# Twelve subtractions of the first batch on GpSimd, and the last accumulators stored in halves

## The chip, the cores and the metric

The kernel runs on one core of one Trainium2 chip. The core has five engines that run their own instruction streams and wait for each other by semaphores: TensorE (PE, matmuls; PEld is its weight load), VectorE (DVE), ScalarE (ACT), GpSimd (POOL) and SyncE (SP, here only a queue of transfers). Matmuls write to PSUM, all else works in SBUF. The metric is the device time of one execution in microseconds (us). Lower is better.

## The reference

A two-sided attention between tokens and a small state, and a two-layer network behind it. Cut to what matters:

```python
scores = scale * x @ state.T                  # 8 batches, 8 heads, 512 tokens, 32 states, 64 wide
xread  = softmax(scores)  @ state             # for each token
sread  = softmax(scale * state @ x.T) @ x     # for each state
t = concatenate([xread, sread], axis=2)       # 8 x (512 + 32) rows of 512
h = t @ w_in                                  # 512 -> 2048
g = where(h >= 1, h, where(h <= -1, 0, (h + 1) ** 2 / 4))
out = g @ w_out                               # 2048 -> 512
```

All of it is in float32.

## The kernel before, in words

**Tiling.** The network is done in 9 passes: one for the 512 tokens of each of 8 batches, and a last one (`b == B`) for the 256 state rows of all batches. A pass has 8 steps `j` (the last pass 4), each for 256 of the 2048 hidden columns. In a step, `g1` makes two `h` tiles of 128 x 512 in PSUM, from the attention weights and `sw`, which is the state times a chunk of W_in (so `xread` is never formed). ScalarE and VectorE turn `h` into the hidden values `u`: relu (L482), square (L485), bound (L488). `g2` of the step before then multiplies hidden values by W_out and adds into four accumulators `acc`.

**High and low parts.** For float32 accuracy each operand of a matmul is kept as a high part, rounded to the matmul's type by ScalarE, and a low part, which is the value minus the high part. Each product is then three matmuls: high by high, high by low, low by high (L534 to L536 in `g2`). The low parts are subtractions with two inputs: `Hidden.low` for the hidden values (`gl`, L502, both inputs in SBUF), `part_low` for W_out (`wol`, L607, both in SBUF), `sw_low` for `sw` (L436, one input in PSUM), `Attention.rest` (L306).

**The first batch is crowded.** During pass 0 the weights arrive too. Each of the 8 chunks of W_in and 8 tiles of W_out comes in a form that has to be put together: two casts, `high` (L588, ScalarE) and `low` (L575 on VectorE or L580 on ScalarE, as the planner picks), and a `join` (L596, VectorE, both inputs in SBUF). A tile of W_out is then split by `part_high` (L603, ScalarE) and `part_low` (L607). The attention of batches 0 and 1 runs there as well. Between the steps on TensorE stand, one for each step, the transposes and products of the attention's second side (`e2p`, `sr`, `rt`, `sc`), which share with `sw` the single PSUM tile called `mm`. The tile `u` exists once, so a step's relu waits until `gl` of the step before has been made. `gl` and `gh` exist twice.

**What sets the order.** Pass 0 is written as a list of operations, each with engine, a cost, what it comes after, and which buffers it takes. The class `Plan` plays that list forward by its costs, always starting the ready operation with the longest tail behind it, and `emit` writes out the instructions in the order of the planned starts. An engine then runs them strictly in this order. TensorE's order and that of the loads on SP are as written. From pass 1 on the code's own order holds, and nothing of it is changed but the end.

**The end.** After the last step, `store(B, t)` copies each of the two accumulators of the last pass to SBUF (t = 0 on ScalarE, L549; t = 1 on VectorE, L547) and writes it out in four transfers of 32 rows, two from SP and two from ScalarE's queue (L556).

Of the kernel before, what the change touches and what calls it, by code (L numbers as in the profile page):

```python
# [8 lines left out]
F32 = mybir.dt.float32  # L9
# [4 lines left out]
ALU = mybir.AluOpType  # L14
# [8 lines left out]
class Plan:  # L23
# [1 line left out]

    LATE = {"SP": 3.9, "PE": 0.3, "ACT": 0.12, "DVE": 0.12}

    def __init__(self, room, turns, bias):  # L30
        self.bias = bias
# [5 lines left out]
    def op(self, key, engine, cost, run, after=(), take=(), ends=()):  # L37

        after = list(after)
        prior = self.last.get(engine) if engine in ("PE", "SP") else None  # L40
        self.last[engine] = key
        self.ops[key] = [engine, cost, run, after, list(take), list(ends), prior]

    def late(self, k):
        return self.LATE[self.ops[k][0].split("/")[0]]

# [32 lines left out]
    def times(self):  # L79
# [6 lines left out]
        free = dict(self.room)  # L86
        begun, done, where, idle = {}, {}, {}, {e: 0.0 for e in self.LATE}
        events = set()
# [49 lines left out]
def state_exchange_moe(  # L138
# [17 lines left out]
    nc = tc.nc  # L156
    B, P, NT, H, D = x.shape
    S = NT * P
    NS = 32
    DM = H * D  # L160
# [6 lines left out]
    TOK = S + NS  # L167
# [283 lines left out]
    acc = {}  # L451

    class Hidden:
# [39 lines left out]
        def high(self):  # L493
            b, j = self.b, self.j
            gh = work.tile([P, 2, S], F32R, tag="gh", name=f"gh{b}_{j}")
            gl = work.tile([P, 2, S], F32R, tag="gl", name=f"gl{b}_{j}")
            nc.scalar.copy(out=gh, in_=self.u)  # L497
            gs[b, j] = (gh, gl)

        def low(self):  # L500
            gh, gl = gs[self.b, self.j]
            nc.vector.tensor_tensor(out=gl, in0=self.u, in1=gh.bitcast(F32), op=ALU.subtract)  # L502

    def g1(b, j):
        hid = Hidden(b, j)
# [9 lines left out]
    def g2(b, j, half=None):  # L515
        n = n_of[b]
        per = S // n
        nt = n // P
        if b not in acc:
            acc[b] = [ps_acc(f"acc{b}_{t}") for t in range(nt)]  # L520
        gh, gl = gs[b, j]
        last = j == NJ // per - 1
        pairs = [(i, t) for i in range(2 * per) for t in range(nt)]
        if last:
            pairs.sort(key=lambda p: p[1])
        if half is not None:
            pairs = pairs[half * len(pairs) // 2:][:len(pairs) // 2]
        for i, t in pairs:
            f = 2 * per * j + i
            oh, ol = wo[f // 2][:, 0, f % 2], wo[f // 2][:, 1, f % 2]  # L530
            c0 = (i % per) * n + t * P
            lh, ll = (v[:, i // per, c0:c0 + P] for v in (gh, gl))
            a = acc[b][t]
            nc.tensor.matmul(a, lhsT=lh, rhs=oh, start=f == 0, stop=False)  # L534
            nc.tensor.matmul(a, lhsT=lh, rhs=ol, start=False, stop=False)  # L535
            nc.tensor.matmul(a, lhsT=ll, rhs=oh, start=False, stop=f == NF - 1)  # L536
            if last and i == 2 * per - 1:
                store(b, t)
# [3 lines left out]
    def store(b, t):  # L542
        if t == 0:
            outs[b] = rawp.tile([P, NT, DM], F32, tag="raw", name=f"o{b}")
        o = outs[b][:, t]
        if b == B and t % 2:
            nc.vector.tensor_copy(o, acc[b][t])  # L547
        else:
            nc.scalar.copy(out=o, in_=acc[b][t])  # L549
        if b < B:  # L550
            r0 = b * TOK + t * P
            nc.scalar.dma_start(out=out[r0:r0 + P, :], in_=o)
        else:
            for i in range(4):
                r0 = (4 * t + i) * TOK + S
                (nc.sync if i % 2 else nc.scalar).dma_start(  # L556
                    out=out[r0:r0 + NS, :], in_=o[i * NS:(i + 1) * NS]
                )

# [1 line left out]
    parts = {}  # L563
# [26 lines left out]
    def join(kind, c):  # L590
        raw = raws[kind, c]
        if kind == "i":
            a = w32[c].rearrange("p k f -> p (k f)")
        else:
            a = parts[c] = work.tile([P, 1024], F32, tag="tmp", name=f"wf{c}")
        nc.vector.scalar_tensor_tensor(  # L596
            out=a.bitcast(I32), in0=raw[..., 1], scalar=3, in1=raw[..., 0],
            op0=ALU.logical_shift_left, op1=ALU.bitwise_or,
        )

    def part_high(c):
        wo[c] = wop.tile([P, 2, 2, DM], F32R, tag="wo", name=f"wo{c}")
        nc.scalar.copy(out=wo[c][:, 0].rearrange("p a c -> p (a c)"), in_=parts[c])  # L603

    def part_low(c):
        wh, wl = (wo[c][:, i].rearrange("p a c -> p (a c)") for i in range(2))
        nc.vector.tensor_tensor(out=wl, in0=parts[c], in1=wh.bitcast(F32), op=ALU.subtract)  # L607

# [2 lines left out]
    op = plan.op  # L613

    def read(key, cost, f, *a, take=(), after=()):
        op(("dma",) + key, "SP", cost, lambda: f(*a), after=after, take=take)
# [4 lines left out]
    def chunk_ops(c):  # L621

        k = ("i", c)
        read(k, 2.6, fetch, "i", c, take=[("raw", k)])
        op(("high",) + k, "ACT", 1.05, lambda: high("i", c), [("dma",) + k])
        op(("low",) + k, "ACT/DVE", (1.15, 0.75), lambda e: low("i", c, e), [("dma",) + k])
        op(("w", c), "DVE", 1.14, lambda: join("i", c), [("high",) + k, ("low",) + k], ends=[k])

    def out_ops(c):

        k = ("o", c)
        read(k, 2.6, fetch, "o", c)
        op(("high",) + k, "ACT", 1.05, lambda: high("o", c), [("dma",) + k])
        op(("low",) + k, "ACT/DVE", (1.15, 0.75), lambda e: low("o", c, e), [("dma",) + k])
        op(("join", c), "DVE", 1.14, lambda: join("o", c), [("high",) + k, ("low",) + k], take=[("tmp", k)])
        op(("woh", c), "ACT", 0.95, lambda: part_high(c), [("join", c)], ends=[k])
        op(("wol", c), "DVE", 1.14, lambda: part_low(c), [("woh", c)], ends=[k])

    atts = {}

# [46 lines left out]
    hid = {}  # L687

    def hidden_ops(b, j):
        k = (b, j)  # L690
        for i in range(2):
            op(("relu", i) + k, "ACT", 0.58, lambda i=i: hid[k].relu(i), [("p", i) + k], ends=[("h", i) + k],
               take=[("u", ("u",) + k)] if i == 0 else [])
        op(("square",) + k, "ACT", 0.97, lambda: hid[k].square(), [("relu", 0) + k, ("relu", 1) + k])
        for i in range(2):
            op(("bound", i) + k, "DVE", 0.6, lambda i=i: hid[k].bound(i), [("square",) + k], ends=[("h", i) + k])
        op(("gh",) + k, "ACT", 0.97, lambda: hid[k].high(), [("bound", 0) + k, ("bound", 1) + k],
           ends=[("u",) + k], take=[("g", ("g",) + k)])
        op(("gl",) + k, "DVE", 1.14, lambda: hid[k].low(), [("gh",) + k], ends=[("u",) + k])

    def tensor(key, cost, f, after=(), take=(), ends=()):
        op(key, "PE", cost, f, after, take, ends)
# [35 lines left out]
    chunk_ops(0)  # L738
    chunk_ops(1)
    out_ops(0)  # L740
    read(("sb", 1), 1.2, lambda: nc.sync.dma_start(out=sb[:, 1:], in_=state[:, 1:]))
    read(("xn", 0), 2.6, load, "xn", load_xn, 0, take=[("xn", ("xn", 0))])
    chunk_ops(2)
    out_ops(1)
    read(("xt", 1), 2.6, load, "xt", load_xt, 1, take=[("xt", ("xt", 1))])
    for c in range(3, NC):
        chunk_ops(c)
        out_ops(c - 1)
        if c == 5:
            read(("xn", 1), 2.6, load, "xn", load_xn, 1, take=[("xn", ("xn", 1))])  # L750
# [4 lines left out]
    for side in range(2):  # L755
        tensor(("sc", 0, side), 0.6, lambda side=side: att_start(0, side), [("dma", "xt", 0, side)],
               ends=[("xt", 0)])
# [18 lines left out]
    for j in range(NJ):  # L776
        g1_ops(0, j)
        hidden_ops(0, j)
        if j + 1 < NC:
            sw_ops(0, j + 1, 1)  # L780
        if j:
            g2_ops(0, j - 1, 0)
        if j in between:
            between[j]()
        if j == 2:
            att_ops1(1)
            att_ops2(1)
        if j:
            g2_ops(0, j - 1, 1)
# [79 lines left out]
```

## Time and profile before

| | |
|---|---|
| time, median of 3 runs | 663.96 us (663.55 to 664.05) |
| the profiled execution | 664.0 us, its span on the core 662.2 us |
| granted TensorE clock | 1.00 |
| GpSimd | 0.8 us busy, 7 instructions, the last at 1.1 us |
| first `g2` matmul | 29.68 us after the span's start |
| first `sw` matmul of batch 1 | 94.17 us |
| last matmul begins | 657.64 us |
| last copy | 658.07 us, 0.69 long |

How to read it: times inside the profile count from the span's start. A row of a timeline gives start, duration, engine, line, operation, output and inputs, and shape. Instructions of one engine overlap a little at their ends, so the distance from start to start is shorter than the duration. Something in brackets is idle time in front of the instruction and what ended it. The profile's busy time of TensorE holds modelled ends.

### The profile page before, as it was taken

Reading aid. Unit: us, or ns where it says so; the run is one execution under the profiler, and the core shown is the slowest. Engines: PE = TensorE matmul, PEld = TensorE weight load, DVE = VectorE, ACT = ScalarE, POOL = GpSimd, SP = SyncE. Lnnn points to the kernel's source line nnn. Section 1 sums busy time; section 2 is a strip of 40 time slices with the busy share of each in tenths; the row PEclk is TensorE's granted clock in tenths of the full one; section 3 lists DMA queues with packets and bytes.
Section 4 is the critical chain, followed back from the end, with each engine's and each line's share of the span. In section 5 each row is a group of like instructions: output and inputs, shape, how many; then the busy total and the mean of one; then the engine's idle time right before and its main releaser. Section 6 shows DMA issues by size and latency. Waiting matters only on the chain.

```text
span 662.2 us, 10304 instructions
## 1 busy us (share of the span) xinstructions
PE 653.9 (99%) x4442; PEld 514.2 (78%) x4442; DVE 340.3 (51%) x490; ACT 356.5 (54%) x462; POOL 0.8 (0%) x7
## 2 busy tenths in 40 slices
PE   8999999999999999999999999999999999999997
PEld 6677777777787777777787777777778777778896
DVE  5999947623673239433563338433563343333431
ACT  4899847544554446544554447444653454454642
POOL 0000000000000000000000000000000000000000
PEclk9999999999999999999999999999999999999999
DMA  8986103010301003010301002010100000000101
GB/s 359 400 359 249 64 10 119 0 65 0 120 10 64 1 4 124 0 65 0 128 1 64 1 24 105 0 65 0 65 1 1 1 33 32 1 1 1 63 1 33
DMA packets 11085, 43.65 MB, mean 66 GB/s; under 512 B 1312, under 2 KB 1440, under 8 KB 7968
## 3 DMA queue, kind: packets, MB, share of 16 engines
q1 hardware_dynamic: 6096, 34.28, 13.6%
q10 hardware_dynamic: 4944, 8.72, 3.5%
q8 instruction: 35, 0.57, 0.3%
q14 instruction: 10, 0.08, 0.0%
HBM read 34.08 MB, written 8.91 MB: 65 GB/s over the span
## 4 chain that ended last, share of the span: by engine, by line
PE 91%; ACT 5%; DVE 3%; issue 0%; DMA 0%; POOL 0%; SPq 0%; ACTq 0%; POOLq 0%
PE acc L534 19%; PE acc L536 18%; PE acc L535 18%; PE h L477 9%; PE h L479 9%; PE h L478 9%; PE sw L417 5%; PE sc L253 1%; PE sr L350 1%; PE e2p L333 1%; PE warmed L198 1%; ACT u L482 1%; ACT u L485 1%; ACT raw_i L588 1%; DVE w L596 1%; ACT wo L603 0%
## 5 line engine op out<-in xcount | busy, mean ns | idle before, releaser
L534 PE MATMUL acc<-wo,gh 128*128 128x512 f32 x544 | 218.8, 402 | 0.0
L535 PE MATMUL acc<-wo,gh 128*128 128x512 f32 x544 | 212.3, 390 | 0.0
L536 PE MATMUL acc<-wo,gl 128*128 128x512 f32 x544 | 212.2, 390 | 0.0
L482 ACT ACTIVATE u<-h,half 128x512 f32<-128x512 f32 x136 | 93.7, 693 | 219.9 <-PE h L479 202.6
L488 DVE SCALAR_TENSOR_TENSOR u<-u,h 128x512 f32<-128x512 f32 x136 | 87.0, 680 | 206.7 <-ACT u L485 206.7
L534 PEld LDWEIGHTS acc<-wo,gh 128*128 128x128 f32 x544 | 102.1, 188 | 40.1 <-ACT u L482 12.8
L536 PEld LDWEIGHTS acc<-wo,gl 128*128 128x128 f32 x544 | 102.1, 188 | 22.5 <-issue 0.4
L535 PEld LDWEIGHTS acc<-wo,gh 128*128 128x128 f32 x544 | 102.2, 188 | 19.4 <-DVE wo L607 0.3
L502 DVE TENSOR_TENSOR gl<-u,gh 128x1024 fp32r<-128x1024 f32 x68 | 83.2, 1224 | 33.0 <-ACT gh L497 32.0
L497 ACT CAST gh<-u 128x1024 fp32r<-128x1024 f32 x68 | 71.8, 1056 | 50.3 <-DVE u L488 49.9
L485 ACT ACTIVATE u<-u 128x1024 f32<-128x1024 f32 x68 | 72.5, 1065 | 1.3
L417 PE MATMUL sw<-w,sb 64*32 64x256 f32 x1024 | 36.0, 383 | 1.8 <-DVE w L596 1.3
L417 PEld LDWEIGHTS sw<-w,sb 64*32 64x32 f32 x1024 | 15.1, 106 | 17.9 <-issue 8.8
L479 PE MATMUL h<-atl,sw_0h 128*128 128x512 f32 x60 | 23.6, 393 | 0.3 <-DVE atl L306 0.2
L477 PE MATMUL h<-ath,sw_0h 128*128 128x512 f32 x60 | 23.5, 394 | 0.0
L549 ACT COPY o<-acc 128x512 f32<-128x512 f32 x33 | 18.6, 586 | 9.1 <-PE acc L536 9.0
L478 PE MATMUL h<-ath,sw_0l 128*128 128x512 f32 x60 | 23.5, 391 | 0.0
L479 PE MATMUL h<-atl,sw_6h 128*128 128x512 f32 x60 | 23.4, 389 | 0.0
L479 PE MATMUL h<-atl,sw_2h 128*128 128x512 f32 x60 | 23.4, 389 | 0.0
L477 PE MATMUL h<-ath,sw_2h 128*128 128x512 f32 x60 | 23.3, 389 | 0.0
L478 PE MATMUL h<-ath,sw_2l 128*128 128x512 f32 x60 | 23.3, 389 | 0.0
L477 PE MATMUL h<-ath,sw_4h 128*128 128x512 f32 x60 | 23.3, 389 | 0.0
(174 smaller groups left out, 735.0 us busy)
## 6 DMA issues: line engine op xcount, KB each, us to landing
xt<-in_xt_dram SPq DMA_DIRECT2D x16, 512.0 KB, 4.5
raw_i<-in_moe_w_in_dram SPq DMA_DIRECT2D x8, 1024.0 KB, 6.9
raw_o<-in_moe_w_out_dram SPq DMA_DIRECT2D x8, 1024.0 KB, 9.4
xn<-in_x_dram SPq DMA_DIRECT2D x8, 1024.0 KB, 6.4
out_dram<-o ACTq DMA_DIRECT2D x32, 256.0 KB, 2.0
sb<-in_state_dram SPq DMA_DIRECT2D x1, 448.0 KB, 12.6
out_dram<-o SPq DMA_DIRECT2D x4, 64.0 KB, 1.7
out_dram<-o ACTq DMA_DIRECT2D x4, 64.0 KB, 2.0
```

The source lines that it names most:

```text
L417: nc.tensor.matmul(pt[pr * NS:(pr + 1) * NS, hh, i * CI:(i + 1) * CI], lhsT=sb[rows, b, pr], rhs=w32[c + i][rows, pr], start=True, stop=True,)
L477: nc.tensor.matmul(o, lhsT=wh[:, k, sl], rhs=ah[:, k], start=first, stop=False)
L478: nc.tensor.matmul(o, lhsT=wl[:, k, sl], rhs=ah[:, k], start=False, stop=False)
L479: nc.tensor.matmul(o, lhsT=wh[:, k, sl], rhs=al[:, k], start=False, stop=last)
L482: nc.scalar.activation(out=self.u[:, i], in_=self.hs[i], func=AF.Relu, scale=0.5, bias=half)
L485: nc.scalar.activation(out=self.u, in_=self.u, func=AF.Square)
L488: nc.vector.scalar_tensor_tensor(out=self.u[:, i], in0=self.u[:, i], scalar=1.0, in1=self.hs[i], op0=ALU.min, op1=ALU.max,)
L497: nc.scalar.copy(out=gh, in_=self.u)
L502: nc.vector.tensor_tensor(out=gl, in0=self.u, in1=gh.bitcast(F32), op=ALU.subtract)
L534: nc.tensor.matmul(a, lhsT=lh, rhs=oh, start=f == 0, stop=False)
L535: nc.tensor.matmul(a, lhsT=lh, rhs=ol, start=False, stop=False)
L536: nc.tensor.matmul(a, lhsT=ll, rhs=oh, start=False, stop=f == NF - 1)
```

## The change

It has two parts.

The first: in pass 0 the low parts of all 8 W_out tiles (`part_low`) and of the hidden values of every second step (`low` for j = 1, 3, 5, 7) are computed by GpSimd instead of VectorE. The planner gets GpSimd as a fifth engine, with a cost of 2.3 for each of these and 0.15 as the time until others see the result. Since the planner works from costs, much of the order of pass 0 on ScalarE and VectorE is laid anew.

The second: each of the two last accumulators is copied in two halves of 256 columns, one by ScalarE and one by VectorE, and each half is written out by a single transfer of 128 rows, one from ScalarE's queue and one from SP's.

```diff
-    LATE = {"SP": 3.9, "PE": 0.3, "ACT": 0.12, "DVE": 0.12}
+    LATE = {"SP": 3.9, "PE": 0.3, "ACT": 0.12, "DVE": 0.12, "POOL": 0.15}
...
         def low(self):
             gh, gl = gs[self.b, self.j]
-            nc.vector.tensor_tensor(out=gl, in0=self.u, in1=gh.bitcast(F32), op=ALU.subtract)
+            engine = nc.gpsimd if self.b == 0 and self.j % 2 else nc.vector
+            engine.tensor_tensor(out=gl, in0=self.u, in1=gh.bitcast(F32), op=ALU.subtract)
...
         o = outs[b][:, t]
-        if b == B and t % 2:
-            nc.vector.tensor_copy(o, acc[b][t])
-        else:
+        if b < B:
             nc.scalar.copy(out=o, in_=acc[b][t])
-        if b < B:
             r0 = b * TOK + t * P
             nc.scalar.dma_start(out=out[r0:r0 + P, :], in_=o)
         else:
-            for i in range(4):
-                r0 = (4 * t + i) * TOK + S
-                (nc.sync if i % 2 else nc.scalar).dma_start(
-                    out=out[r0:r0 + NS, :], in_=o[i * NS:(i + 1) * NS]
-                )
+            rows = out.rearrange("(b t) d -> b t d", b=B)[4 * t:4 * t + 4, S:S + NS]
+            lo, hi = slice(0, DM // 2), slice(DM // 2, DM)
+            nc.scalar.copy(out=o[:, lo], in_=acc[b][t][:, lo])
+            nc.vector.tensor_copy(o[:, hi], acc[b][t][:, hi])
+            nc.scalar.dma_start(out=rows[:, :, lo], in_=o[:, lo])
+            nc.sync.dma_start(out=rows[:, :, hi], in_=o[:, hi])
...
     def part_low(c):
         wh, wl = (wo[c][:, i].rearrange("p a c -> p (a c)") for i in range(2))
-        nc.vector.tensor_tensor(out=wl, in0=parts[c], in1=wh.bitcast(F32), op=ALU.subtract)
+        nc.gpsimd.tensor_tensor(out=wl, in0=parts[c], in1=wh.bitcast(F32), op=ALU.subtract)
...
-        op(("wol", c), "DVE", 1.14, lambda: part_low(c), [("woh", c)], ends=[k])
+        op(("wol", c), "POOL", 2.3, lambda: part_low(c), [("woh", c)], ends=[k])
...
-        op(("gl",) + k, "DVE", 1.14, lambda: hid[k].low(), [("gh",) + k], ends=[("u",) + k])
+        op(("gl",) + k, "POOL" if j % 2 else "DVE", 2.3 if j % 2 else 1.14, lambda: hid[k].low(), [("gh",) + k], ends=[("u",) + k])
```

The line numbers after the change are one lower for the lines behind `store` (L588 becomes L587, L596 becomes L595, L603 becomes L602, L607 becomes L606) and one higher for those between `low` and `store` (L502 becomes L503, L534 to L536 become L535 to L537).

GpSimd's queue after its start-up rows, all of it new. `wo` is the low part of a W_out tile (0 to 7 in this order), `gl` that of the hidden values of step 1, 3, 5 or 7, `wf` a joined tile:

```order
L606 TENSOR_TENSOR wo_276<-wf_247,wo_276 128x1024
L606 TENSOR_TENSOR wo_364<-wf_357,wo_364 128x1024
L503 TENSOR_TENSOR gl_1_420<-u_1_300,gh_1_419 128x1024
L606 TENSOR_TENSOR wo_446<-wf_434,wo_446 128x1024
L606 TENSOR_TENSOR wo_485<-wf_478,wo_485 128x1024
L606 TENSOR_TENSOR wo_609<-wf_588,wo_609 128x1024
L503 TENSOR_TENSOR gl_3_627<-u_3_533,gh_3_626 128x1024
L606 TENSOR_TENSOR wo_643<-wf_630,wo_643 128x1024
L606 TENSOR_TENSOR wo_714<-wf_688,wo_714 128x1024
L606 TENSOR_TENSOR wo_736<-wf_724,wo_736 128x1024
L503 TENSOR_TENSOR gl_5_813<-u_5_716,gh_5_812 128x1024
L503 TENSOR_TENSOR gl_7_943<-u_7_898,gh_7_942 128x1024
```

`gl` of step 3 stands behind the low part of W_out tile 4, which step 4 needs.

ScalarE at the end of step 0, before, from the high cast of W_in chunk 2 (`raw_i_198`) on; `gh_0` is the high part of step 0, `wo` that of W_out tile 0, `e` the copy of `e2p`, `u_1` the relus of step 1:

```order
L588 ACTIVATE raw_i_198<-raw_i_198 128x1024
L497 CAST gh_0_306<-u_0_222 128x1024
L603 CAST wo_310<-wf_247 128x1024
L337 COPY e_0_237<-e2p_286 128x1024
L482 ACTIVATE u_1_298<-h_1_0_299,half 128x512
L482 ACTIVATE u_1_298<-h_1_1_312,half 128x512
L432 CAST sw_2h<-sw_2_327 128x512
L485 ACTIVATE u_1_298<-u_1_298 128x1024
```

and after:

```order
L602 CAST wo_276<-wf_247 128x1024
L587 ACTIVATE raw_i_198<-raw_i_198 128x1024
L497 CAST gh_0_309<-u_0_222 128x1024
L337 COPY e_0_237<-e2p_287 128x1024
L587 ACTIVATE raw_o_208<-raw_o_208 128x1024
L432 CAST sw_2h<-sw_2_327 128x512
L482 ACTIVATE u_1_300<-h_1_0_301,half 128x512
L482 ACTIVATE u_1_300<-h_1_1_313,half 128x512
L602 CAST wo_364<-wf_357 128x1024
L485 ACTIVATE u_1_300<-u_1_300 128x1024
```

The cast of W_out tile 0 now comes first, and that of tile 1 (`wo_364`) stands in front of the square of step 1.

VectorE behind the bound of step 1 (the L488 pair on `u_1`), before; `wf` and `w` are joins of W_out tiles and W_in chunks, L575 the `low` casts:

```order
L488 SCALAR_TENSOR_TENSOR u_1_298<-u_1_298,h_1_1_312 128x512
L596 SCALAR_TENSOR_TENSOR wf_399<-raw_o_208 128x1024
L596 SCALAR_TENSOR_TENSOR w_3_90<-raw_i_268 128x1024
L502 TENSOR_TENSOR gl_1_402<-u_1_298,gh_1_401 128x1024
L607 TENSOR_TENSOR wo_417<-wf_399,wo_417 128x1024
L358 TENSOR_TENSOR rs_433<-sr_366,r_0_323 128x128
L575 TENSOR_SCALAR raw_i_320<-raw_i_320 128x1024
L596 SCALAR_TENSOR_TENSOR wf_446<-raw_o_295 128x1024
L596 SCALAR_TENSOR_TENSOR w_4_91<-raw_i_320 128x1024
```

and after:

```order
L488 SCALAR_TENSOR_TENSOR u_1_300<-u_1_300,h_1_1_313 128x512
L595 SCALAR_TENSOR_TENSOR w_3_90<-raw_i_268 128x1024
L358 TENSOR_TENSOR rs_422<-sr_367,r_0_321 128x128
L595 SCALAR_TENSOR_TENSOR wf_434<-raw_o_296 128x1024
L574 TENSOR_SCALAR raw_i_325<-raw_i_325 128x1024
L574 TENSOR_SCALAR raw_o_360<-raw_o_360 128x1024
L595 SCALAR_TENSOR_TENSOR w_4_91<-raw_i_325 128x1024
L595 SCALAR_TENSOR_TENSOR wf_478<-raw_o_360 128x1024
L436 TENSOR_TENSOR sw_3l<-sw_3_453,sw_3h 128x512
```

The two subtractions are gone, the joins have closed up, and a `low` cast of W_out tile 3 that ScalarE did has come over.

VectorE behind the bound of step 3, after:

```order
L488 SCALAR_TENSOR_TENSOR u_3_533<-u_3_533,h_3_1_547 128x512
L574 TENSOR_SCALAR raw_o_541<-raw_o_541 128x1024
L275 TENSOR_TENSOR z_492<-z_492,m_1_493 128x512
L595 SCALAR_TENSOR_TENSOR wf_630<-raw_o_541 128x1024
L574 TENSOR_SCALAR raw_i_568<-raw_i_568 128x1024
L271 TENSOR_REDUCE m_1_493<-z_492 128x16
L595 SCALAR_TENSOR_TENSOR w_7_94<-raw_i_568 128x1024
```

where two joins, `gl` of step 3 and the low part of W_out tile 4 stood before. L275 and L271 are the first side of batch 1's attention, moved up.

## The prediction

> **What bounds the kernel now.** I read the page first, then the busy time by stretches, then the chain that ended last, then the rows of each engine in the stretch in question. The page says TensorE, and that GpSimd is unused:
>
> ```profile
> PE 653.9 (99%) x4442; PEld 514.2 (78%) x4442; DVE 340.3 (51%) x490; ACT 356.5 (54%) x462; POOL 0.8 (0%) x7
> ```
>
> The average hides the first batch. The columns below are stretch, its length, and busy us of PE, PEld, DVE, ACT, POOL, then clock and DMA:
>
> ```profile
> 21.00:35.00 14.00, 13.06 (x152) 9.32 (x151) 13.39 (x20) 13.85 (x20) 0.00 (x0) 1.00 0.94 379
> 35.00:50.00 15.00, 14.98 (x97) 10.56 (x103) 14.03 (x20) 14.19 (x19) 0.00 (x0) 1.00 0.93 373
> 50.00:62.00 12.00, 12.00 (x79) 8.96 (x80) 11.62 (x14) 12.00 (x16) 0.00 (x0) 1.00 0.84 330
> 62.00:80.00 18.00, 17.86 (x168) 13.39 (x166) 17.90 (x30) 15.12 (x19) 0.00 (x0) 1.00 0.18 60
> ```
>
> In these 59 us VectorE is busy for 13.39 + 14.03 + 11.62 + 17.90 = 56.9. TensorE is dense as well, so three engines are full at once, and every us by which VectorE or ScalarE hands over later moves the rest of the program, in which TensorE is never idle. The chain of waits shows how tight it is; it leaves VectorE for good only here:
>
> ```profile
> 60.45 1.10 DVE wf L596
> 61.55 0.55 issue
> 62.10 0.69 DVE sw_5l L436
> ```
>
> There is little to win. From the first `g2` on, TensorE waits twice, about 0.3 us each: for the low part of W_out 0 (the page's row of that matmul's weights names it last), and at 62.84.
>
> ```profile
> L535 PEld LDWEIGHTS acc<-wo,gh 128*128 128x128 f32 x544 | 102.2, 188 | 19.4 <-DVE wo L607 0.3
> ```
>
> So what counts is whether the new order delivers on time.
>
> **GpSimd's price.** No row shows a subtraction on GpSimd. The nearest of its own rows, and VectorE's rows for the work itself:
>
> ```profile
> 1.10 0.29 POOL masks.py:199 TENSOR_SCALAR_AFFINE_SELECT ident<-ident 128x128 f32<-128x128 f32 x1
> ```
> ```profile
> 25.75 0.69 DVE L575 TENSOR_SCALAR raw_o<-raw_o 128x1024 int32<-128x1024 uint32 x1
> 26.36 1.22 DVE L596 SCALAR_TENSOR_TENSOR w<-raw_i 128x1024 int32<-128x1024 int32 x1
> 27.49 1.22 DVE L502 TENSOR_TENSOR gl<-u,gh 128x1024 fp32r<-128x1024 f32 x1
> ...
> 28.91 1.20 DVE L607 TENSOR_TENSOR wo<-wf,wo 128x1024 fp32r<-128x1024 f32 x1
> ```
>
> Eight times the 128 columns of the first row are 0.29 x 8 = 2.3 us with one input; with two, at worst, 4.6. From below, VectorE's own 1.22. I take **2.3**, the row of the same engine. The Trainium skill (GPSIMD Engine Reference, Performance versus the Vector engine) gives 4497 ns for 2048 elements of a two-input add; half of that is an estimate of 2.25 us, which no run here shows yet.
>
> **Do the two engines get in each other's way?** No row of before has both computing at once. What VectorE's rows show, from start to start: 1024 elements with one input take 26.36 - 25.75 = 0.61 us, with two inputs 27.49 - 26.36 = 1.13 us. Input elements go by at the same rate, so VectorE already draws two streams from SBUF in both forms. I take it as likelier that a third reader has to wait its turn than that it has a way of its own. So my forecast is that a GpSimd subtraction and a VectorE instruction of those two kinds (two SBUF inputs, or the fast one-input form) **take turns**, each whole. Instructions that read PSUM (L436, L488), reductions and transposes go on beside GpSimd. The Trainium skill says the same of this change (SBUF — State Buffer, Who interferes with whom): a VectorE instruction with two SBUF inputs, or in a two-port mode, and a GpSimd instruction that reads SBUF exclude each other for the whole instruction, whoever starts first. By that rule the subtractions cost more than they save; whether it holds here, only the next trace can show.
>
> **The change, place by place, with turns.** I lay the new orders out with the durations of before. Twelve subtractions leave VectorE (12 x 1.13 = 13.6 us). The planner also gives VectorE four `low` casts that ScalarE did (0.61 each, against 1.12 from start to start on ScalarE, 55.61 to 56.73 below).
>
> *Place A, step 0.*
>
> ```profile
> 25.06 1.20 ACT L588 ACTIVATE raw_i<-raw_i 128x1024 f32<-128x1024 f32 x1
> 26.10 1.08 ACT L497 CAST gh<-u 128x1024 fp32r<-128x1024 f32 x1
> 27.04 1.08 ACT L603 CAST wo<-wf 128x1024 fp32r<-128x1024 f32 x1
> ```
> ```profile
> 29.09 0.67 PE L417 MATMUL sw<-w,sb 64*32 64x256 f32 x16 [0.45 <-ACT e L337]
> ...
> 30.51 0.40 PE L536 MATMUL acc<-wo,gl 128*128 128x512 f32 x1
> ```
>
> The cast of W_out tile 0 now goes first: 25.06 + 1.08 = 26.14. GpSimd lets the fast cast at 25.75 end (26.44) and holds until 28.74. VectorE's join of `w` 2 is ready at 27.2 (cast, then 1.2 for the input), but starts at 28.74 and ends at 29.9, so `sw` 2 moves from 29.09 to 29.95. `gl(0,0)` follows at 30.2 (two small rows, 0.3) and ends at 31.4, wanted at 30.51. **A = +0.9.**
>
> *Place B, `gl(0,1)`.* After `gl(0,0)` VectorE does a fast cast and the join of `wf` 1 (30.2 + 1.13 + 0.61 + 1.2 = 33.1); only then can ScalarE cast W_out tile 1 (34.2), and the square of step 1 now stands behind that cast. GpSimd holds from 34.2 to 36.5. Then VectorE has a run without a gap: `w` 3, a 0.2 us row, `wf` 2, two fast casts, `w` 4, `wf` 3 = 4 x 1.13 + 0.2 + 2 x 0.61 = 5.9, to 42.4. `gh(0,1)` is ready about 38.3, so `gl(0,1)` on GpSimd waits for the end of the run: 42.4 to 44.7. It is wanted by this matmul, moved by A:
>
> ```profile
> 40.74 0.40 PE L536 MATMUL acc<-wo,gl 128*128 128x512 f32 x1
> ```
>
> 40.74 + 0.9 = 41.6. **B = +3.1.** Behind it on GpSimd wait the low parts of tiles 2 and 3; the single `u` tile stays taken, so ScalarE's relu of step 2 waits too.
>
> *The transpose at 53.39.* ScalarE now has a `low` cast in front of `sw_4h`:
>
> ```profile
> 51.40 0.61 ACT L432 CAST sw_4h<-sw 128x512 fp32r<-128x512 f32 x1
> ...
> 54.58 1.20 ACT L588 ACTIVATE raw_o<-raw_o 128x1024 f32<-128x1024 f32 x1
> 55.61 1.31 ACT L580 ACTIVATE raw_o<-raw_o,offset 128x1024 int32<-128x1024 uint32 x1
> 56.73 1.11 ACT L497 CAST gh<-u 128x1024 fp32r<-128x1024 f32 x1
> ```
> ```profile
> 52.35 0.68 DVE L436 TENSOR_TENSOR sw_4l<-sw,sw_4h 128x512 fp32r<-128x512 f32 x1
> ```
> ```profile
> 53.39 0.27 PE L364 MATMUL rt<-ident,rs 128*128 128x128 f32 x1
> ```
>
> It delays `sw_4l` by 1.1; the `mm` tile came free at 52.35 + 0.68 = 53.03, 0.36 before its next user. **+0.7**, with turns or without.
>
> *Place C, `gl(0,3)`.* GpSimd's queue has the low part of W_out 4 ahead of it. That cast now stands where ScalarE was at 54.58; moved by 0.9 + 3.1 + 0.7 = 4.7 it ends at 60.4, GpSimd holds until 62.7, VectorE's run (fast cast, subtract of 512 columns, join, fast cast: 0.61 + 0.6 + 1.13 + 0.61) lasts until 65.7, `gl(0,3)` until 68.0. Wanted here:
>
> ```profile
> 60.24 0.40 PE L536 MATMUL acc<-wo,gl 128*128 128x512 f32 x1
> ...
> 62.31 0.39 PE L536 MATMUL acc<-wo,gl 128*128 128x512 f32 x1
> 62.84 1.09 PE L333 MATMUL e2p<-ident,e 128*128 128x128 f32 x8
> ```
>
> 60.24 + 4.7 = 64.9: 3.0 late, of which 0.3 replaces the wait at 62.84 (matmuls of this form follow each other every 0.23, so this one could have begun at 62.54). **C = +2.7.**
>
> *Place D, the `mm` tile for `sr(1)`.* From the end of `gl(0,3)`, T, VectorE does a join, a fast cast, then while GpSimd holds (2.3) only `sw_5l`, then a fast cast, a join (to T + 5.8), the pair of L488 with two small rows (7.4), and subtract, sum, join, `gl(0,4)` (10.9). GpSimd holds until T + 13.2; then normalise, 0.3 of small rows, transpose, `sw_6l`: T + 15.4. TensorE needs the tile at:
>
> ```profile
> 72.89 1.10 PE L350 MATMUL sr<-xn,e 128*32 128x64 f32 x64
> ```
>
> That is 72.89 - 60.24 - 0.3 = 12.35 after T. **D = +3.0.** Later GpSimd subtractions (steps 5 and 7) come behind the loads and joins, where VectorE has gaps again, and have slack.
>
> *The tail.* Columns of the DMA rows: minimum, median and maximum ns of an issue, first and last start; then us to landing, of L556 and of L552.
>
> ```profile
> 7.21 0.78 DVE L260 STREAM_TRANSPOSE z<-sc 128x256 f32<-128x256 f32 x2 [6.31 <-PE sc L253]
> ...
> 658.07 0.69 DVE L547 COPY o<-acc 128x512 f32<-128x512 f32 x1 [5.42 <-DMA out_dram<-o]
> ```
> ```profile
> L556 SPq DMA_DIRECT2D out_dram<-o x4: 315/386/415, 656.0 to 659.2; - x4
> DMA to landing us min/median/max: 1.6/1.9/2.0
> ```
> ```profile
> DMA to landing us min/median/max: 2.0/2.0/4.3
> ```
>
> The last copy shrinks from 0.69 to about 0.4 (the 256-wide rows), and each queue issues one transfer for the last tile instead of two: the last issue moves from 659.2 to 658.55. A transfer of 128 rows lands in 2.0 (L552) against 1.9. So -0.65 + 0.15 = **-0.5** (bounds -0.8, and +0.5 if 1 KB rows land slower than any row here).
>
> **Sum.** 0.9 + 3.1 + 0.7 + 2.7 + 3.0 - 0.5 = +9.9. The profiled execution took 664.0 us (span 662.2, 1.8 around it), the median of three is 663.96, so either base gives **673.9**. With 1.22 per subtraction about +4.5 remains (668.5); with 4.6 about twice the sum.
>
> **Rivals.**
> 1. *Side by side, no turns* (not slower). A: the low part of W_out 0 is done at 26.2 + 2.3 = 28.5, and TensorE's wait for it goes, -0.3; `gl(0,1)` is in time; the transpose +0.7; C: tile 4 at 55.0 to 56.1, its low part to 58.4, `gl(0,3)` to 60.7, wanted at 60.64, so +0.1, less 0.3; D up to +0.4; tail -0.5: between -0.3 and +0.1, **664.0**. It decides if a subtraction on GpSimd lasts about 2.3 while VectorE's rows stay at 1.13. For it: VectorE is relieved of 13.6 us. At 4.6 us each, `gl(0,3)` alone would be 4.7 late.
> 2. *Turns, but GpSimd always gets in first.* Eleven subtractions before 82 us hold VectorE for 25.3; it is relieved of 11 x 1.13 = 12.4 and given 2.4 of casts: +15.3, and VectorE was full. **678.8.**
> 3. *Only GpSimd waits, VectorE is never held.* A -0.3; B +2.5 (the run starts 1.5 earlier and the demand 1.2 earlier); transpose +0.7; C +0.5; D +0.5; tail -0.5: **667.4.**
> 4. *A real gain*: all waits of TensorE (0.6) and the tail at its best (0.8) are won: **662.5.** It needs a GpSimd about as fast as VectorE.
>
> **How the numbers follow.** A run of this kernel can tell 0.2% (1.3 us) from nothing. Forecast 0.36, rival 2 0.16, rival 3 0.16, rival 1 0.28, rival 4 0.04. Slower: 0.36 + 0.16 + 0.16, and 0.03 of rival 1 with a slower GpSimd = 0.71; same 0.25; faster 0.04. The range runs from rival 1's lower part, 663.6, to 681, rival 2 with a somewhat longer subtraction. The forecast's own range is 668.5 to 678.
>
> **What would show it.** Turns: VectorE rows of L595, L503 or L574 that last 2 to 3 us where a GpSimd row overlaps them, and PE waits on `gl` at about 42 and 65 us of 3 us each. Side by side: those rows stay at 1.22 and 0.69, and `sw` of batch 1 starts at about 94 as before. The tail: one issue per queue after the last copy, its end 0.5 closer to the last matmul. The forecast is wrong if GpSimd rows lie over two-input VectorE rows without either growing.

## The result: slower by 2.8%, and the profile after

The changed kernel takes 682.08 us (681.52 to 683.1, five runs), the kernel before beside it 663.96 us. The ratio is 1.0282, with a 95% interval of 1.0269 to 1.0295 (the two medians alone give 1.0273). The profiled execution took 682.88 us, its span is 681.1 us. The direction was as forecast; the time is 8.2 us above the forecast of 673.9 and 1.1 us above the upper end of its range. One execution of a later kernel, `e1_tail_only`, took 3701.75 us with TensorE slow throughout, and its figure leaves that execution out.

First the page's line of busy times after the change, in us, with shares of the span and counts:

```profile
PE 658.3 (97%) x4442; PEld 517.4 (76%) x4442; DVE 347.0 (51%) x483; ACT 353.2 (52%) x459; POOL 33.2 (5%) x19
```

Twelve subtractions left VectorE, 12 x 1.13 = 13.6 us by the rows of before, and yet its busy time rose from 340.3 to 347.0. That is the first thing to look into. VectorE's and GpSimd's rows in one stretch after the change (start, duration, engine, line, operation, output and inputs, shape):

```profile
61.52 2.63 DVE L574 TENSOR_SCALAR raw_o<-raw_o 128x1024 int32<-128x1024 uint32 x1
64.08 2.85 DVE L275 TENSOR_TENSOR z<-z,m 128x512 f32<-128x512 f32 x1
...
70.32 2.85 DVE L574 TENSOR_SCALAR raw_o<-raw_o 128x1024 int32<-128x1024 uint32 x1
```
```profile
61.19 2.42 POOL L606 TENSOR_TENSOR wo<-wf,wo 128x1024 fp32r<-128x1024 f32 x1 [11.33 <-ACT wo L602]
63.56 2.82 POOL L503 TENSOR_TENSOR gl<-u,gh 128x1024 fp32r<-128x1024 f32 x1
69.23 3.39 POOL L606 TENSOR_TENSOR wo<-wf,wo 128x1024 fp32r<-128x1024 f32 x1 [2.85 <-ACT wo L602]
```

The cast of L574 takes 0.69 us by itself, the subtraction of L275 0.68. Here each lasts until the GpSimd row beside it is over (61.19 + 2.42 = 63.61) and then does its own work. So the engines do take turns, each whole. But it is VectorE that stands still inside its run of work. The second GpSimd row starts at 63.56, in the middle of a run of VectorE: GpSimd didn't wait for a gap.

Where TensorE waited, from 20 to 112 us after the change (waiting instruction, what released it; us in total, times, longest):

```profile
PE e2p L333 <- DVE sw_5l L436: 4.8, 1, 4.8
PE sc L253 <- DVE sw_3l L436: 3.4, 1, 3.4
PE sr L350 <- DVE sw_6l L436: 2.4, 1, 2.4
PE sw L417 <- DVE r L339: 1.3, 1, 1.3
PE acc L537 <- POOL gl L503: 0.8, 1, 0.8
```

Three of the waits are for `sw_3l`, `sw_5l` and `sw_6l`, VectorE's subtractions out of PSUM (which VectorE reads as well as SBUF, L436 and L488) that set the single `mm` tile free for the second attention, that of batch 1. Only 0.8 us is a wait for GpSimd's own result, and in this stretch VectorE and ScalarE wait for none. The first `sw` matmul of batch 1 begins at 110.65 us against 94.17: of the 18.9 us by which the span grew, 16.5 are lost in the first batch. The other 2.4 are at the end: from the start of the last tile's first copy to the end of the span were 662.2 - 658.1 = 4.1 us, and now 681.1 - 674.6 = 6.5:

```profile
674.17 0.39 PE L537 MATMUL acc<-wo,gl 128*128 128x512 f32 x1
674.60 0.37 ACT L554 COPY o<-acc 128x256 f32<-128x256 f32 x1 [2.35 <-PE acc L537]
675.00 0.55 ACTq L556 DMA_DIRECT2D out_dram<-o  x1
675.00 0.42 DVE L555 COPY o<-acc 128x256 f32<-128x256 f32 x1 [2.29 <-ACT o L554]
675.46 0.54 SPq L557 DMA_DIRECT2D out_dram<-o  x1
```

Each copy is shorter, as forecast, but the two run one behind the other. So the last issue starts 675.46 - 674.17 = 1.29 us after the last matmul starts, against 659.2 - 657.64 = 1.56 before: 0.3 us are gained. That issue is over at 676.0, and the writes themselves then take until about 679.5.

The trace also shows TensorE's clock at half behind the long waits. Busy us in two pieces after the wait for `sc` (stretch, length, then PE, PEld, DVE, ACT, POOL, clock, DMA share, GB/s):

```profile
46.90:48.00 1.10, 1.02 (x16) 0.23 (x16) 0.62 (x2) 1.10 (x2) 0.52 (x1) 0.50 0.75 313
48.00:50.00 2.00, 2.00 (x19) 0.94 (x4) 1.50 (x4) 1.41 (x2) 1.86 (x1) 0.50 1.03 434
```

`sc` takes 1.96 us in place of 1.09. So from the trace alone there are four suspects: the turns, the new order of the planner, the halved clock, and the writes at the end.

### The profile page after: what moved, and what is told of

It reads as the page before. It is cut to its first block, busy times and chain, and to the rows that moved or that the text cites. A ratio compares the mean times of both kernels' runs of the same rounds, so it can differ in the third digit from the quotient of the medians.

```text
span 681.1 us, 10318 instructions
## 1 busy us (share of the span) xinstructions
PE 658.3 (97%) x4442; PEld 517.4 (76%) x4442; DVE 347.0 (51%) x483; ACT 353.2 (52%) x459; POOL 33.2 (5%) x19
## 4 chain that ended last, share of the span: by engine, by line
PE 87%; DVE 8%; ACT 2%; issue 2%; POOL 0%; ACTq 0%; DVEq 0%; POOLq 0%
PE acc L535 18%; PE acc L537 17%; PE acc L536 17%; PE h L477 9%; PE h L479 9%; PE h L478 9%; PE sw L417 4%; DVE w L595 1%; DVE wf L595 1%; PE sr L350 1%; PE sc L253 1%; DVE raw_o L574 1%; PE e2p L333 1%; PE warmed L198 1%; DVE gl L503 1%
## 5 line engine op out<-in xcount | busy, mean ns | idle before, releaser
L535 PE MATMUL acc<-wo,gh 128*128 128x512 f32 x544 | 220.1, 405 | 0.0
L537 PE MATMUL acc<-wo,gl 128*128 128x512 f32 x544 | 213.1, 392 | 0.8 <-POOL gl L503 0.8
L536 PE MATMUL acc<-wo,gh 128*128 128x512 f32 x544 | 213.3, 392 | 0.0
L488 DVE SCALAR_TENSOR_TENSOR u<-u,h 128x512 f32<-128x512 f32 x136 | 87.1, 680 | 208.5 <-ACT u L485 208.5
L535 PEld LDWEIGHTS acc<-wo,gh 128*128 128x128 f32 x544 | 102.9, 189 | 41.0 <-ACT u L482 12.8
L537 PEld LDWEIGHTS acc<-wo,gl 128*128 128x128 f32 x544 | 102.7, 189 | 24.4 <-POOL gl L503 1.2
L536 PEld LDWEIGHTS acc<-wo,gh 128*128 128x128 f32 x544 | 102.9, 189 | 19.2
L503 DVE TENSOR_TENSOR gl<-u,gh 128x1024 fp32r<-128x1024 f32 x64 | 80.5, 1258 | 33.6 <-ACT gh L497 32.6
L606 POOL TENSOR_TENSOR wo<-wf,wo 128x1024 fp32r<-128x1024 f32 x8 | 21.7, 2722 | 54.4 <-ACT wo L602 54.4
L477 PE MATMUL h<-ath,sw_6h 128*128 128x512 f32 x60 | 23.4, 389 | 0.0
```

The lines of the kernel that those rows point to most:

```text
L477: nc.tensor.matmul(o, lhsT=wh[:, k, sl], rhs=ah[:, k], start=first, stop=False)
L488: nc.vector.scalar_tensor_tensor(out=self.u[:, i], in0=self.u[:, i], scalar=1.0, in1=self.hs[i], op0=ALU.min, op1=ALU.max,)
L503: engine.tensor_tensor(out=gl, in0=self.u, in1=gh.bitcast(F32), op=ALU.subtract)
```

## The experiments

Differences are against the kernel before on the same chip (663.3 to 663.5 us).

### Order and engine apart

Four kernels. The first has only the change's `store`:

```diff
 # kernel before
-            for i in range(4): ... (32 rows x 512 columns each)
+            nc.scalar.dma_start(out=rows[:, :, lo], in_=o[:, lo])
+            nc.sync.dma_start(out=rows[:, :, hi], in_=o[:, hi])
```

> The kernel before with the change's last copies and writes alone (two halves of 256 columns on two engines, one transfer of 4 x 32 rows of 1 KB for each half). If the trace of the changed kernel is read rightly, the end behind the last matmul grows from 4.1 to 6.4 us, and the time goes from 664.0 to 666.3 (665.8 to 666.8). By the prediction's term for the tail it is 0.5 us faster: 663.5.

Measured: 665.8 us, ratio 1.0031 (1.0019 to 1.0044), so 2.3 us slower by the medians. The second is the changed kernel with the `store` of before:

> The changed kernel with the tail of before: only the twelve subtractions are on GpSimd. If the parts add up, 682.1 - 2.3 = 679.8 (679.0 to 680.6). If the tail costs more or less beside a late first batch, another number.

Measured: 679.64 us, 16.2 slower. 16.2 + 2.3 = 18.5 against 18.1 for the whole change: the parts add up to within 0.4 us. From here on the tail is that of before. The third keeps the new plan but runs its subtractions on VectorE, the fourth keeps the old plan and runs them on GpSimd:

```diff
 # e3: the changed kernel's plan (cost 2.3 on "POOL")
-        nc.gpsimd.tensor_tensor(out=wl, ...)
+        nc.vector.tensor_tensor(out=wl, ...)
 # e4: the plan of before (cost 1.14 on "DVE")
-        nc.vector.tensor_tensor(out=wl, ...)
+        nc.gpsimd.tensor_tensor(out=wl, ...)
 # and gl of steps 1, 3, 5, 7 likewise
```

> The order of instructions that the changed kernel's planner makes, with all twelve subtractions on VectorE again, and the tail of before. Theory of turns: without GpSimd rows no VectorE row is held, VectorE does 1.13 us each as before, so 664 within 1.5 us. Rival, that the new order and not the engine costs the time: 676 or more.

> The order of before, with the twelve subtractions on GpSimd, and the tail of before. Theory of turns: VectorE's rows are held to 2.4 to 3 us beside GpSimd rows here too, and sc, e2p and sr of the second attention come late, so 674 to 684. Rival, that the new order costs the time: 664 to 666.

Measured: 672.39 us (+8.9) and 669.89 us (+6.4). Neither theory had that. The turns alone don't make 16.2 in the old order, and the new order costs time without any GpSimd row. What TensorE waits for with the old order:

```profile
PE sw L417 <- ACT e L322: 1.8, 1, 1.8
PE acc L536 <- POOL wo L608: 0.8, 1, 0.8
```

The others are 0.7 us at most and spread out; none for `e2p` or `sc` is over 0.4 us.

### Shorter holds, a warm clock, no subtractions, and the forms by themselves

All three kernels have the new order and the tail of before. In the first each GpSimd subtraction is cut in four; in the second TensorE has matmuls in front of its three waits (the first column of `pad` holds 0.5, so they add to one row of an accumulator and not only zeros); in the third GpSimd only fills the twelve low parts with zeros, so the subtractions are left out:

```diff
 # e5
-        nc.gpsimd.tensor_tensor(out=wl, in0=parts[c], in1=wh.bitcast(F32), op=ALU.subtract)
+        for q in range(4):
+            s = (slice(None), slice(q * 256, q * 256 + 256))
+            nc.gpsimd.tensor_tensor(out=wl[s], in0=parts[c][s], in1=wh[s].bitcast(F32), op=ALU.subtract)
 # e6
+    nc.tensor.matmul(acc[b][0][:PAD, :P], lhsT=pad, rhs=ident, start=False, stop=False)  # 14, 20, 5 times
 # e7
-        nc.gpsimd.tensor_tensor(out=wl, in0=parts[c], in1=wh.bitcast(F32), op=ALU.subtract)
+        nc.gpsimd.memset(wl.bitcast(F32), 0.0)
```

> The new order and the tail of before, each of the twelve subtractions on GpSimd cut into four of 256 columns. If the two engines take turns by whole instructions, a VectorE row waits for a quarter (0.6 to 0.75 us) and not for 2.4 us: rows that were 2.6 to 3.4 us long fall to 1.3 to 2, and the time falls from 679.6 to 668 to 674. If a GpSimd subtraction slows VectorE by traffic, in whatever pieces, or the new order is the cost, it stays at 678 to 682.

> The subtractions on GpSimd in the new order with the tail of before, and TensorE kept at work where it idled: matmuls that add zeros, 14 ahead of sc, 20 ahead of e2p and 5 ahead of sr of the second attention. If the halved clock behind each idle stretch is a cost of its own, sc, e2p and the matmuls behind them keep a pitch of 0.23 us, and 679.6 falls by some 5 us to 674.5 (673.5 to 676). If that time is covered by something else that is late, 678.5 to 680.

> The new order and the tail of before, with GpSimd filling the twelve low parts with zeros in place of the subtractions, so that the low parts of W_out and of every second step's values in the first batch are left out. Theory of turns: without a two-input GpSimd row no VectorE row is held, and the new order by itself costs nothing: 664 within 1.5 us. Rival, that the order of the new planner costs the time (672.4 with all on VectorE): 670 or more. If a fill holds VectorE as a subtraction does, for its shorter time: 665 to 669, with VectorE rows of 1.5 to 2.2 us beside it.

Measured: quarters 675.66 us (+12.4), warm 679.5 us, no subtractions 665.14 us (+1.9).

The third shows that with VectorE really relieved the new order costs only 1.9 us. (A fill is also done sooner than a subtraction, but in the changed kernel only 0.8 us was a wait for a GpSimd result.) The first shows that the length of the single GpSimd instruction matters, though less than expected: TensorE now waits 1.7 us for a `gl` from GpSimd. The second refutes the clock as a cost. The busy times of `e2_subs_only` by stretch, then those of `e6_warm`:

```profile
36.00:52.00 16.00, 12.57 (x69) 8.05 (x68) 14.67 (x16) 10.72 (x14) 8.33 (x3) 0.79 0.83 329
52.00:74.00 22.00, 17.17 (x100) 12.42 (x99) 20.88 (x19) 17.25 (x22) 8.61 (x3) 0.97 0.49 192
74.00:88.00 14.00, 12.76 (x79) 9.75 (x80) 13.90 (x19) 7.80 (x10) 5.77 (x2) 0.80 0.00 1
```
```profile
36.00:52.00 16.00, 15.69 (x108) 12.09 (x107) 14.69 (x16) 10.80 (x14) 8.34 (x3) 1.00 0.87 343
52.00:74.00 22.00, 19.64 (x132) 14.92 (x131) 21.07 (x21) 17.15 (x22) 8.58 (x3) 1.00 0.46 183
74.00:88.00 14.00, 11.42 (x96) 8.68 (x98) 13.90 (x19) 7.80 (x10) 5.75 (x2) 1.00 0.00 1
```

The clock went from 0.79, 0.97 and 0.80 to 1.00 in all three stretches, and `sr` begins at 87.61 us in place of 87.74. VectorE's column explains it: 14.67 of 16 us, 20.88 of 22, 13.90 of 14, and nearly the same in `e6_warm`. VectorE, its held time included, is the bound through these 52 us. What TensorE won by its clock went into the added matmuls and into new waits, of which two for `gl` are 1.1 and 1.0 us.

The fourth kernel measures the turns by themselves: ten forms on VectorE, three of each, first alone, then beside GpSimd's subtractions, fills and copies of 1024 columns.

```python
# v = VectorE, g = GpSimd; tiles of 128 x 1024, pq in PSUM (512), tiny 16 columns
L37 v.tensor_tensor(vo, va, vb)          L38 the same, 512 columns
L39 v.tensor_scalar(vo, va)              L40 v.tensor_scalar(tiny, tiny)
L41 v.tensor_tensor(vo, pq, va), 512     L43 v.transpose(vo, pq), 512
L64 g.tensor_tensor(go, ga, gb)          L65 g.memset(go)          L66 g.tensor_copy(go, ga)
```

> No part of the reference is computed: ten forms of VectorE instruction, three of each, first alone, then beside GpSimd subtractions of 1024 columns, then beside GpSimd fills, then beside GpSimd copies. By the traces so far, beside subtractions: two SBUF inputs 1.13 and 0.6 us grow to 3 to 3.5, one SBUF input (1024 and 16 columns) to 2.4 to 3; PSUM input, reduction and transposes keep their 0.6 to 0.7. A rival, that everything on VectorE is held: all ten forms by over 1 us. Beside fills: nothing is held, if only GpSimd's reads take the turn.

Its timeline of VectorE, three instructions to a row: alone, then beside subtractions (from 29.43), fills (from 116.03) and copies (from 159.15). Then GpSimd's rows of subtractions and fills:

```profile
3.53 3.73 DVE L37 TENSOR_TENSOR vo<-va,vb 128x1024 f32<-128x1024 f32 x3
7.29 2.15 DVE L38 TENSOR_TENSOR vo<-va,vb 128x512 f32<-128x512 f32 x3
9.47 2.15 DVE L39 TENSOR_SCALAR vo<-va 128x1024 f32<-128x1024 f32 x3
11.53 0.59 DVE L40 TENSOR_SCALAR tiny<-tiny 128x16 f32<-128x16 f32 x3
12.03 2.13 DVE L41 TENSOR_TENSOR vo<-pq,va 128x512 f32<-128x512 f32 x3
...
29.43 8.20 DVE L38 TENSOR_TENSOR vo<-va,vb 128x512 f32<-128x512 f32 x3
37.67 8.20 DVE L39 TENSOR_SCALAR vo<-va 128x1024 f32<-128x1024 f32 x3
45.79 4.74 DVE L40 TENSOR_SCALAR tiny<-tiny 128x16 f32<-128x16 f32 x3
50.45 2.13 DVE L41 TENSOR_TENSOR vo<-pq,va 128x512 f32<-128x512 f32 x3
...
116.03 3.75 DVE L37 TENSOR_TENSOR vo<-va,vb 128x1024 f32<-128x1024 f32 x3
...
121.99 3.77 DVE L39 TENSOR_SCALAR vo<-va 128x1024 f32<-128x1024 f32 x3
...
163.65 4.29 DVE L38 TENSOR_TENSOR vo<-va,vb 128x512 f32<-128x512 f32 x3
167.97 4.29 DVE L39 TENSOR_SCALAR vo<-va 128x1024 f32<-128x1024 f32 x3
```
```profile
24.99 90.80 POOL L64 TENSOR_TENSOR go<-ga,gb 128x1024 f32<-128x1024 f32 x36
...
117.36 41.55 POOL L65 MEMSET go<- 128x1024 f32 x40
```

Beside subtractions a VectorE instruction of 0.6 us (L38, L39) comes round every 8.20 / 3 = 2.73 us: 2.1 us of one GpSimd subtraction, then its own 0.6. Neither starves in these two forms: one instruction of each, in turn. The form with a PSUM input is not touched (2.13 and 2.13), nor are reductions and transposes. A fill (41.55 / 40 = 1.04 us each) leaves the two-input form alone (3.75 against 3.73) but holds the fast one-input form by 0.54 us each (3.77 against 2.15). That was not expected of a fill; in `e7_no_subs` such holds sum to 2.0 us (the table below), beside the 1.9 us by which it is slower. The Trainium skill (SBUF — State Buffer, Who interferes with whom) states these pairs: two SBUF inputs against a GpSimd instruction that reads, the two-port forms against any. The runs agree, and add that with both queues full the lock passes to and fro.

### The account of VectorE, tested forward

If VectorE is the bound up to `sw_6l`, its end must follow from what VectorE has to do before it. The table is worked out from the traces: "held" is the sum, over VectorE's rows from 20 us up to the end of `sw_6l`, of what each row is longer than the median row of its form in the kernel before. "Subtractions" are those of `gl` and `wo` that VectorE did itself until then, "casts" the `low` casts it did.

| kernel | order | end of `sw_6l` | held | subtractions | casts |
|---|---|---|---|---|---|
| before | old | 72.31 | 0.2 | 11 | 8 |
| e4, GpSimd | old | 77.39 | 12.4 | 3 | 8 |
| e3, VectorE | new | 80.85 | 0.4 | 13 | 12 |
| e7, fills | new | 73.57 | 2.0 | 3 | 12 |
| e5, quarters | new | 84.16 | 9.6 | 3 | 12 |
| e2, GpSimd | new | 87.68 | 16.9 | 3 | 12 |
| changed kernel | new | 87.87 | 16.9 | 3 | 12 |

From e7 to the changed kernel the end moves by 14.3 us and the held time by 14.9. Until then GpSimd has begun ten subtractions: 1.7 us of VectorE for each, where VectorE does one in 1.13. And the new order has already spent what it counted on: VectorE's own subtractions until `sw_6l` fall from 11 to 3, 8 x 1.13 = 9.0 us, but 71 instructions stand before it and not 67, the planner having put four more casts and a good part of the second attention's softmax there. So the whole held time lands on `sw_6l`. In the old order the 9.0 us stay free: e4's end moves by 5.1 us, 2.7 of them busy time of VectorE up to there (53.0 against 50.3) and 2.4 idle time. The account has a limit: it takes VectorE's idle time as given. That is 2.0 to 4.5 us up to `sw_6l` in six of the seven kernels but 7.2 in e5, whose end moves 3.0 us more against e7 than its held time.

Two kernels test that account: the old order with quarters, and a planner that is told the truth.

```diff
 # e10: kernel before, each subtraction as four of 256 columns on GpSimd (as in e5)
 # e11: the change's subtractions on GpSimd, the tail of before, and
-        op(("wol", c), "POOL", 2.3, lambda: part_low(c), ...)
+        op(("wol", c), "DVE", 1.7, lambda: part_low(c), ...)
 # and gl of odd steps likewise
```

> The order and the tail of before, the twelve subtractions on GpSimd, each in four of 256 columns. By the account of VectorE's time up to sw_6l (held 12.4 us with whole subtractions in this order against 9.1 us taken away; quarters held 9.6 where whole ones held 16.9): held some 7, so 663.5 to 666.5. Rival, that GpSimd's own results come later in quarters and become the wait: 668 or more, with TensorE waiting for wo or gl from GpSimd.

> The subtractions whole on GpSimd and the tail of before, but the planner reckons them as 1.7 us of VectorE (what they cost it by the held rows) in place of 2.3 us of GpSimd. If it is the planner's filling of time that VectorE does not have that puts the products sw late, the conversions stay on ScalarE and the time is 666 to 671 (669.9 with the order of before). If the order does not matter: 678 to 681.

Measured: `e10_old_quarters` 668.43 us (+5.1), `e11_told` 667.63 us (+4.3). In `e11_told` 11.9 of the 16.2 us have gone although the subtractions are on GpSimd as before; `sw_6l` ends at 75.48 with 9.4 us held and 7 casts. VectorE is idle for 8.4 us up to there, so it is no longer the bound throughout. Its waits:

```profile
PE e2p L333 <- DVE sw_5l L436: 0.8, 1, 0.8
PE acc L537 <- DVE gl L503: 0.8, 1, 0.8
PE sr L350 <- DVE sw_6l L436: 0.6, 1, 0.6
```

In `e10_old_quarters` the held time did fall, to 5.8, but the rival came true:

```profile
PE e2p L333 <- DVE sw_5l L436: 2.2, 1, 2.2
PE acc L540 <- POOL wo L614: 1.2, 1, 1.2
```

With quarters GpSimd lets VectorE in between its pieces, so its own results are later (12 quarters in a row took 11.8 us, 3.9 for each subtraction), and TensorE waits 1.2 us for one. The longer wait has the same origin: ScalarE's relu waits 2.4 us for a `gl` from GpSimd, ScalarE's `sw_5h` comes behind that relu, and VectorE's `sw_5l` waits 3.1 us for `sw_5h`. None of these kernels beats the one before.

### The writes at the end

```diff
 # e8: kernel before, copies in halves as in the change, and each half as
+            for i in range(4):
+                nc.scalar.dma_start(out=rows[i, :, lo], in_=o[i * NS:(i + 1) * NS, lo])
+                nc.sync.dma_start(out=rows[i, :, hi], in_=o[i * NS:(i + 1) * NS, hi])
 # e9: kernel before, whole-row copies, and each tile as
+            (nc.sync if t % 2 else nc.scalar).dma_start(out=rows, in_=o)
```

> The kernel before, the last accumulators copied in halves as in the change, but each half written as four transfers of 32 rows of 1 KB. If the change's writes are slow because four blocks of rows in one transfer are shared out over few DMA engines, the DMA share is 0.7 or more here as in the kernel before (0.2 in the changed one), and the time 664 to 665.5, four issues more being the price. If 1 KB rows are slow, the share stays near 0.2 and the last tile takes 2.9 us to write: 666 or more.

> The kernel before with its whole-row copies, each last tile written by one transfer of 4 x 32 rows of 2 KB. If four blocks in one transfer are shared out over few DMA engines, the share is near 0.2, the 256 KB of the last tile take some 2.6 us in place of 1.2, and the time is 664.3 to 665.5. If row size was the cause, the share is 0.7 or more and the time 662.7 to 663.6.

Measured: `e8_tail_eight` 664.54 us, ratio 1.0018 (1.0009 to 1.0027); `e9_tail_full` 668.28 us, ratio 1.0076 (1.0063 to 1.0088). The last tile's write in each, as DMA share and GB/s in the last two columns: the kernel before, the changed one, `e8_tail_eight`, `e9_tail_full`:

```profile
659.50:660.80 1.30, 0.00 (x0) 0.00 (x0) 0.00 (x0) 0.00 (x0) 0.00 (x0) 1.00 0.75 202
```
```profile
676.50:679.50 3.00, 0.00 (x0) 0.00 (x0) 0.00 (x0) 0.00 (x0) 0.00 (x0) 0.79 0.27 95
```
```profile
658.50:660.80 2.30, 0.00 (x0) 0.00 (x0) 0.00 (x0) 0.00 (x0) 0.00 (x0) 0.81 0.42 114
```
```profile
660.50:664.40 3.90, 0.00 (x0) 0.00 (x0) 0.00 (x0) 0.00 (x0) 0.00 (x0) 0.50 0.19 62
```

One transfer of four blocks of 32 rows keeps about a fifth to a quarter of the 16 DMA engines busy, with rows of 1 KB (0.27) and of 2 KB (0.19) alike. So the form of the transfer is the main cause and not the row size. Transfers of 32 rows of 1 KB reach 0.42. The 0.7 that was expected did not show; that the eight issues to a tile spread the transfers out is likely, but was not tried. `e9_tail_full` cost 5.0 us, more than the 1 to 2.2 expected. Its packets show two reasons: a tile of 256 KB takes 4.2 to 4.4 us and not 2.6, and the last tile's write runs behind that of the tile before (656.2 to 660.5 us, then 660.2 to 664.5). In the changed kernel the four transfers likewise run one behind the other, from 673.6 to 679.5. The Trainium skill (DMA: Bandwidth & Descriptors, Why a DMA increments its semaphore by 16 and not by 1) says why a share is low: the number of DMA engines that share a transfer divides the size of the slowest dimension of both sides, so that four blocks get four engines at most. A quarter of 16 agrees with the shares here. So does the count of small packets at the end (under 512 B), in the kernel before, the changed one and `e9_tail_full`:

```profile
DMA packets 385, 0.53 MB, mean 53 GB/s; under 512 B 128, under 2 KB 128, under 8 KB 384
```
```profile
DMA packets 529, 0.53 MB, mean 53 GB/s; under 512 B 16, under 2 KB 528, under 8 KB 528
```
```profile
DMA packets 264, 0.52 MB, mean 44 GB/s; under 512 B 8, under 2 KB 8, under 8 KB 264
```

With 8, 4 and 2 transfers, each transfer of 32 rows has 16 of them, and each of four blocks 4.

## Why the prediction was wrong

**Right**: the change costs time; subtraction and VectorE forms exclude each other for whole instructions, and the PSUM forms, reductions and transposes go free. GpSimd's 2.3 us measures 2.42 where it gets in first (the row at 61.19). Place A was forecast at +0.9: the second `sw` matmul begins at 29.44 against 29.09, in an execution that was 0.5 us ahead (the first `e2p` at 23.84 against 24.35), so +0.9. Place D was forecast as 3.0 us of waiting for the `mm` tile that `sw_6l` sets free; 2.4 was found there, but 1.2 in `e2_subs_only`, whose first batch has the same instructions, so the near agreement is in part luck.

**The step that failed** is the arbitration. The prediction put it as: GpSimd lets VectorE's run end, "so `gl(0,1)` on GpSimd waits for the end of the run: 42.4 to 44.7". The traces and `m1_forms` show an alternation, instruction by instruction. So `gl(0,1)` was done in time and place B did not exist (3.1 forecast, no wait for `gl` there); at C the wait for `gl(0,3)` was 0.8 and not 2.7. The price was paid by VectorE in its runs: `sc` waited 3.4 us for `sw_3l`, and `e2p` 4.8 us for `sw_5l`, which the prediction has no term for. The second rival, GpSimd always first, had the right victim and 678.8 us; the subtractions alone took 679.6. Its rule was not right either, and that its +15.3 comes near the 15.6 us by which `sw_6l` moved is luck: it put the holds at 25.3 us where 16.9 were found up to `sw_6l`, and the relief at 12.4 where 9.0 were found, and it has no term for the softmax rows moved up or for VectorE's idle time.

**The planner** is the other half. I read its order as a given list. That it would spend VectorE's freed time ahead of the `sw` products, so that nothing was left to absorb the holds, was in the instruction lists I had, as four more casts and joins closed up; I didn't price it. `e11_told`, with the same subtractions on GpSimd, puts 12 us on it.

**The transpose at 53.39**, +0.7, did not show: TensorE came later itself, and `sw_4l` was there.

**The clock** stood in no term, and rightly, though I took it for a cost of some 5 us when I saw the trace; `e6_warm` shows it costs nothing while VectorE is the bound.

**The tail** was forecast at -0.5 (bounds -0.8 and +0.5) and is +2.3 by `e1_tail_only`. Of the 0.65 us by which the last issue was to move, 0.3 came, since the two copies run one behind the other, which its 658.55 leaves out. The larger step that failed is "a transfer of 128 rows lands in 2.0 (L552) against 1.9": L552 writes 128 adjacent rows, the new one four blocks, and the nearest row in size was not the nearest in form. (The two medians that it quotes give +0.1, where the sum has +0.15.) From the start of the last issue to the end of the span it is now 681.1 - 675.46 = 5.6 us, before 662.2 - 659.2 = 3.0.

**The sum** was +9.9: 10.4 for the first batch where the subtractions cost 16.2, and -0.5 for the tail where it was +2.3. The range ended at 681 because its upper case was rival 2 with the good tail.

## What to carry to other kernels

Before an instruction moves to GpSimd, ask what VectorE does beside it: here each move freed 1.13 us and took 1.7; only beside PSUM forms, reductions, transposes and a reciprocal of 16 columns did a GpSimd subtraction leave VectorE alone. A planner that is told of an engine's time but not of its interference spends the time twice; charging the victim's engine what it loses won back 11.9 of 16.2 us, though no kernel here beat the one before. And a wait or a slow clock on an engine that isn't the bound is not a loss until a run without it is faster.

## What was not expected of the hardware

- Beside GpSimd's subtractions a `tensor_scalar` of 16 columns can be held like one of 1024: three took 4.74 us in place of 0.59, two of them over 2 us each. A reciprocal of 16 columns was not held (0.82 for three, alone and beside them).
- A GpSimd fill holds VectorE's one-input form (2.15 to 3.77 us for three) but not its two-input form (3.73 and 3.75); a GpSimd copy holds both (4.29 for three of L38 and of L39).
- TensorE's clock fell to half behind idle stretches shorter than expected. In `e4_old_order` it idled for 1.8 us ahead of the `sw` matmul at 52.45 and worked on for 1.1 us before the clock was 0.50 for about 3.4 us (the clock is the third column from the end):

```profile
52.40:53.60 1.20, 1.16 (x18) 0.67 (x19) 1.20 (x2) 1.20 (x2) 0.00 (x0) 1.00 0.31 126
53.60:56.00 2.40, 2.40 (x7) 1.90 (x6) 1.68 (x4) 2.40 (x4) 0.00 (x0) 0.50 0.52 109
56.00:58.00 2.00, 2.00 (x8) 1.56 (x8) 1.32 (x3) 1.29 (x4) 0.00 (x0) 0.75 0.95 401
```

The Trainium skill (TensorE: Matmul & The Clock Gate, Part 1: The HAM clock gate) has the clock halved behind a whole idle window of about 3.4 us. This idle stretch was about half of that, so here the trace differs from the rule as it is put there; why is open. The length of an idle stretch alone doesn't decide it: in `e5_quarters` 2.2 us ahead of `sc` at 46.22 left the clock at 1.00.
